# Reordering the beginning of a one-core Fourier-mixing and feed-forward kernel: store count, load order, and where a weight conversion runs

## The chip, the cores and the metric

One core of one Trainium2 chip runs the program. The metric is the device time of one execution in microseconds, lower is better. All runs quoted were in the fast state (in some executions of a program the chip shows a slower one). The kernel before takes 2857.4 us (median).

## The reference

Eight sequences of 3008 x 256 are filtered in the frequency domain; the result, 24064 rows, passes a feed-forward layer with a hard-swish.

```python
X = np.fft.rfft(x, axis=1)                       # x: (8, 3008, 256)
y = np.fft.irfft(X * (filt_r + 1j * filt_i)[None], n=3008, axis=1)
h = y.reshape(24064, 256) @ w_in                 # w_in: (256, 2048), float64
g = h * np.clip(h + 3.0, 0.0, 6.0) / 6.0
out = (g @ w_out).astype(np.float32)             # w_out: (2048, 256), float64
```

## The kernel before

The Fourier transform is done in two matmul stages, through two buffers in memory, z and g. For sequence 0 nothing can overlap, so the program begins with a prologue:

- **Stage A**: eight chunks of x are loaded (`x_load`), multiplied (`a_unit`), copied from PSUM (the memory that matmuls write) by ScalarE and stored to z (`z_store`).
- **Stage B**: z is read back (`t2_load`); twelve units of a matmul, the filter product in five VectorE instructions (`f_unit`, `y_unit`) and an inverse matmul (`bi_unit`); the result goes to g (`g_store`).
- **Bridge**: g is read back (`t4_load`), 40 matmuls (`n_unit`), the first up-projection.
- **Main loop**: 376 steps (47 blocks x 8 weight parts), each an up-projection, hard-swish and down-projection. The stages A and B of sequences 1 to 7 are strewn into it.

The weights arrive as 64-bit floats and are converted to 32 bits by integer instructions on VectorE, then scaled and combined on GpSimd (`w_conv`): sixteen pieces, two per weight part, the pieces of part p being needed by steps p and p + 1.

```python
def w_conv(i):                                   # ... hi, lo: the words of the 64-bit floats
    v.tensor_scalar(out=big, in0=hi, scalar1=3, scalar2=0x3FFFFFFF, ...)
    v.tensor_scalar(out=rest, in0=hi, scalar1=30, scalar2=30, ...)
    v.tensor_tensor(out=big, in0=rest, in1=big, op=ALU.bitwise_or)
    v.tensor_scalar(out=hi, in0=hi, scalar1=20, scalar2=0x7FF, ...)
    v.tensor_scalar(out=hi.bitcast(FP32), in0=hi, scalar1=897.0, op0=ALU.is_ge)
    # ... four more on VectorE; then on GpSimd a product and four sums
def z_store(b, c, q=None):
    # ... for g in range(2): for ri in range(2):
            for h in range(2):                   # 8 stores of 48 KB per chunk
                q.dma_start(z[:, h, ds(c * XC + 2 * g, 2), :], t[p0:p0 + KH, h, :, :])
# ... prologue:
for c in range(NB):                              # stage A
    a_unit(0, c)
    z_store(0, c, nc.scalar)
    if c + 3 < NB: x_load(0, c + 3)
    if c < 4: convert(1)                         # convert: w_conv, then the load of the next piece but one
for c in range(TB):
    table_load(0, c)                             # six loads, 1 MB
    t2_load(0, c, nc.gpsimd)
# ... stage B: convert(1) in every fourth unit
for i in range(2): t4_load(i)                    # eight loads of 120 KB
# ... n_unit x4
for i in range(NCONV - done): at(i // 2, convert, 1)   # nine left: two in each step
```

Of the kernel before, what the change touches and what calls it, by code (L numbers as in the profile page):

```python
# [10 lines left out]
FP32 = mybir.dt.float32  # L11
I32 = mybir.dt.int32
AXT = mybir.ActivationFunctionType
ALU = mybir.AluOpType
# [7 lines left out]
NC = 64  # L22
KH = 24
NF = N // 2 + 1
P = 128
# [4 lines left out]
HC = NC // 2  # L30
XC = 4
NB = HC // XC
TC = 4
NT = KH // TC
TB = 3
# [3 lines left out]
BLK = 512  # L39
NBLK = B * N // BLK  # L40
NJ = 5
RING = 3 * BLK


# [33 lines left out]
def kernel(  # L78
# [9 lines left out]
    nc = tc.nc  # L88
# [9 lines left out]
    g_d = nc.dram_tensor("g_tmp", (B, KH, P, D), FP32, kind="Internal").ap()  # L98

    def pool(name, bufs, **kw):  # L100
        return ctx.enter_context(tc.tile_pool(name=name, bufs=bufs, **kw))

    const = pool("const", 1)
# [11 lines left out]
    op = pool("op", 2)  # L115
# [6 lines left out]
    xs = [const.tile([P, XC, D], FP32, name="xs%d" % i) for i in range(3)]  # L122
    ft = [const.tile([P, TC, D], FP32, name="ft%d" % i) for i in range(TB)]
    t4 = [const.tile([P, NJ, D], FP32, name="t4%d" % i) for i in range(2)]
    xn = const.tile([P, 2, RING], FP32, name="xn")
    w_in = [const.tile([P, 7, P], FP32, name="w_in%d" % p) for p in range(NP)]
    w_out = [const.tile([P, 7, P], FP32, name="w_out%d" % p) for p in range(NP)]
    half_c = const.tile([P, 1], FP32, name="half_c")

    st = {}  # L130

    def raw(src, row, ap):
        return bass.AP(tensor=src.tensor, offset=src.offset + row * D, ap=ap)


    def table_load(b, c):
        t = ft[(b * NT + c) % TB]
        for src, p0 in ((filt_r, 0), (filt_i, HALF)):
            nc.sync.dma_start(t[p0:p0 + 32, :, :].rearrange("p k d -> p (k d)"),
                              raw(src, c * TC, [[NA * D, 32], [1, TC * D]]))  # L140
            nc.sync.dma_start(t[p0 + 32:p0 + 64, :, :], raw(src, NA - c * TC, [[NA * D, 32], [-D, TC], [1, D]]))
        wb = tabp.tile([P, TC, P], FP32, name="wb")
        nc.sync.dma_start(wb, wb_d[:, ts(c, TC), :])
        wi = tabp.tile([P, TC, P], FP32, name="wi")
        nc.sync.dma_start(wi, wi_d[:, ts(c, TC), :])
        st["tab", b, c] = wb, wi
# [8 lines left out]
    def w_part(i):  # L155
        p = i // 2
        if i % 2 == 0:
            cols = ts(p, 256)
            src = moe_w_in[:, cols].bitcast(I32)
            return src.rearrange("(a p) d -> p a d", p=P), w_in[p][:, 0:4, :].rearrange("p (a j) m -> p a (j m)", a=2)  # L160
        src = moe_w_out[ts(p, 2 * P), :].bitcast(I32)
        return src.rearrange("(a p) d -> p a d", p=P), w_out[p][:, 0:4, :].rearrange("p (a j) m -> p a (j m)", a=2)

    def w_load(i):
        if i >= NCONV:
            return
        t = op.tile([P, 1024], I32, name="bits", tag="o")
        nc.gpsimd.dma_start(t.rearrange("p (a d) -> p a d", a=2), w_part(i)[0])
        st["bits", i] = t

    def w_conv(i):
        if i >= NCONV:
            return
        words = st.pop(("bits", i)).rearrange("p (n two) -> p n two", two=2)
        lo, hi = words[:, :, 0], words[:, :, 1]
        big, rest = (sp.tile([P, 2, D], FP32, name=s).bitcast(I32).rearrange("p a n -> p (a n)")
                     for s in ("s1", "s2"))
        v = nc.vector
        v.tensor_scalar(out=big, in0=hi, scalar1=3, scalar2=0x3FFFFFFF,
                        op0=ALU.logical_shift_left, op1=ALU.bitwise_and)  # L180
        v.tensor_scalar(out=rest, in0=hi, scalar1=30, scalar2=30,  # L181
                        op0=ALU.logical_shift_right, op1=ALU.logical_shift_left)
        v.tensor_tensor(out=big, in0=rest, in1=big, op=ALU.bitwise_or)  # L183
        v.tensor_scalar(out=hi, in0=hi, scalar1=20, scalar2=0x7FF,
                        op0=ALU.logical_shift_right, op1=ALU.bitwise_and)
        v.tensor_scalar(out=hi.bitcast(FP32), in0=hi, scalar1=897.0, scalar2=None, op0=ALU.is_ge)
        v.tensor_scalar(out=rest, in0=big, scalar1=23, scalar2=23,
                        op0=ALU.logical_shift_right, op1=ALU.logical_shift_left)
        v.tensor_scalar(out=lo, in0=lo, scalar1=9, scalar2=0x3F800000,
                        op0=ALU.logical_shift_right, op1=ALU.bitwise_or)  # L190
        rest, big = rest.bitcast(FP32), big.bitcast(FP32)
        v.scalar_tensor_tensor(out=rest, in0=lo.bitcast(FP32), scalar=1.0, in1=rest,  # L192
                               op0=ALU.subtract, op1=ALU.mult)
        v.scalar_tensor_tensor(out=rest, in0=rest, scalar=2.0 ** -20, in1=big, op0=ALU.mult, op1=ALU.add)  # L194
        two = lambda t: t.rearrange("p (a d) -> p a d", a=2)
        nc.gpsimd.tensor_tensor(out=w_part(i)[1], in0=two(rest), in1=two(hi.bitcast(FP32)), op=ALU.mult)

        w = (w_in, w_out)[i % 2][i // 2]
        for o, x0, x1, op_ in IN_SUMS if i % 2 == 0 else OUT_SUMS:
            nc.gpsimd.tensor_tensor(out=w[:, o, :], in0=w[:, x0, :], in1=w[:, x1, :], op=op_)  # L200
# [36 lines left out]
            nc.scalar.activation(out=t[:, h, :, :], in_=ps[h], func=AXT.Copy)  # L237
        st["t1", b, c] = t

    def z_store(b, c, q=None):  # L240
        q = q or nc.gpsimd
        t = st.pop(("t1", b, c))
        for g in range(2):
            for ri in range(2):
                p0 = g * 64 + ri * 32
                z = z_d[b, :, ts(ri, NC), :].rearrange("k (h j) d -> k h j d", h=2)
                for h in range(2):
                    q.dma_start(z[:, h, ds(c * XC + 2 * g, 2), :], t[p0:p0 + KH, h, :, :])  # L248

    def t2_load(b, c, q=None):  # L250
        q = q or nc.sync
        t = t2p.tile([P, TC, D], FP32, name="t2")
        q.dma_start(t, z_d[b, ts(c, TC), :, :].rearrange("k p d -> p k d"))
        st["t2", b, c] = t
# [38 lines left out]
    def g_store(b, c, q=None):  # L293
        q = q or nc.gpsimd
        q.dma_start(g_d[b, ts(c, TC), :, :].rearrange("k p d -> p k d"), st.pop(("t3", b, c)))



    chunks = [(b, j, min(NJ, HC - j)) for b in range(B) for j in range(0, HC, NJ)]

# [1 line left out]
        b, j, n = chunks[i]  # L302
        return b * N + j * TOK, n * TOK

    def t4_load(i):
        b, j, n = chunks[i]
        for h in range(2):
            for ri in range(2):
                p0 = h * 64 + ri * 32
                nc.sync.dma_start(t4[i % 2][p0:p0 + KH, 0:n, :], g_d[b, :, ds(ri * NC + h * HC + j, n), :])  # L310


    def n_unit(i, dh):
# [5 lines left out]
        while done < n:  # L319
            o = (t + done) % RING  # L320
            m = min(n - done, RING - o)
            nc.scalar.activation(out=xn[:, dh, ds(o, m)], in_=ps[:, ds(done, m)], func=AXT.Copy)  # L322
# [144 lines left out]
    def at(step, fn, *a):  # L467
        plan.setdefault((step, fn in EARLY), []).append((fn, a))

    with tc.manual_schedule():  # L470



        nc.vector.memset(half_c, 0.5)
        for t in xs:
            nc.gpsimd.memset(t, 0.0)
        nc.sync.dma_start(wa, wa_d)
        for c in range(3):
            x_load(0, c)
# [4 lines left out]
        def convert(n):  # L484
            nonlocal done
            for _ in range(n):
                w_conv(done)
                w_load(done + 2)
                done += 1

        for c in range(NB):
            a_unit(0, c)
            z_store(0, c, nc.scalar)
            if c + 3 < NB:
                x_load(0, c + 3)
            if c < 4:
                convert(1)
        for c in range(TB):
            table_load(0, c)
            t2_load(0, c, nc.gpsimd)  # L500
        nc.sync.dma_start(wai, wai_d)
        for t in t4:
            nc.gpsimd.memset(t, 0.0)
        for i in range(NU + 1):
            if i < NU:
                b_unit(0, i)
                f_unit(0, i)
                y_unit(0, i)
                if i % 4 == 2:
                    convert(1)  # L510
            if i:
                bi_unit(0, i - 1)
                if i % 2 == 0:
                    c = i // 2 - 1
                    g_store(0, c, nc.scalar)
                    if c + TB < NT:
                        table_load(0, c + TB)
                        t2_load(0, c + TB, nc.gpsimd)
        for i in range(2):
            t4_load(i)  # L520
        for i in range(2):
            for dh in range(2):
                n_unit(i, dh)
# [1 line left out]
            x_load(1, c)  # L525

        for i in range(NCONV - done):
            at(i // 2, convert, 1)

        n_at = {0: -2, 1: -2}  # L530
        used = {}
# [131 lines left out]
```

## Time and profile before

| stretch of the trace | from, us | length, us | what fills it |
|---|---|---|---|
| stage A | 0 | 62.4 | DMA share 75%, every engine under 42% |
| stage B | 62.4 | 63.0 | VectorE 87% |
| bridge | 125.3 | 24.3 | a store, a load, then matmuls at a granted clock of 0.57 |
| steps 0 to 5 | 149.6 | 85.1 | VectorE 90% |
| the rest | 234.75 | 2620 | TensorE 99% |

The cuts are the first matmul of stage B, the end of its last VectorE result, the first addition into h of the main loop, and the same addition six steps later. In lines of the profile PE is TensorE, PEld its weight loads, DVE VectorE, ACT ScalarE, POOL GpSimd and SP SyncE; a q behind the name (ACTq) marks DMA issues of that queue.

### The profile page before, as it was taken

What the parts mean: (1) busy time and instruction counts of PE and PEld (TensorE: products, weight loads), DVE (VectorE), ACT (ScalarE), POOL (GpSimd) and SP (SyncE); (2) the same over time, 40 slices, a digit from 0 to 9 for tenths busy, and PEclk for the clock granted to TensorE, in tenths of its full rate; (3) what the DMA queues carried; (4) which work ended last, traced back from release to release, by engine and by line L of the source; (5) the groups of instructions that cost most, each with busy time, mean ns of one, the idle gap of its engine ahead of it and who ended that gap; (6) DMA issues with size and microseconds to landing.
All of it is one profiled execution on the core that took longest, in us unless ns stands there. A gap on an engine that the chain in (4) does not pass through costs nothing.

```text
span 2854.4 us, 47635 instructions
## 1 busy us (share of the span) xinstructions
PE 2726.7 (96%) x18096; PEld 2469.4 (87%) x18096; DVE 1995.0 (70%) x3492; ACT 1331.6 (47%) x2670; POOL 511.7 (18%) x836
## 2 busy tenths in 40 slices
PE   4569999999999999999999999999999999999997
PEld 1358988999989999899988999899998999999996
DVE  3687875677756777577765777567775677766665
ACT  1124445544554445544455444554455444444443
POOL 3274003200131001310123010320013100000000
PEclk9789999999999999999999999999999999999998
DMA  6544213421134212332223221332113421110000
GB/s 200 161 128 109 88 39 87 109 82 48 48 87 112 63 51 65 95 102 56 60 69 92 85 79 39 86 107 67 58 45 91 117 66 45 34 32 23 18 8 15
DMA packets 129323, 211.92 MB, mean 74 GB/s; under 512 B 26184, under 2 KB 87240, under 8 KB 129096
## 3 DMA queue, kind: packets, MB, share of 16 engines
q1 hardware_dynamic: 100072, 146.98, 18.5%
q0 software_dynamic: 23552, 55.62, 6.6%
q10 hardware_dynamic: 5472, 6.29, 0.7%
q8 instruction: 143, 2.34, 0.3%
q14 instruction: 84, 0.69, 0.1%
HBM read 133.81 MB, written 74.97 MB: 73 GB/s over the span
## 4 chain that ended last, share of the span: by engine, by line
PE 91%; DVE 5%; DMA 2%; issue 1%; ACT 1%; ACTq 0%; SPq 0%; POOL 0%; POOLq 0%; DVEq 0%
PE po L417 41%; PE al L341 22%; PE be L341 17%; PE psn L316 4%; PE psf L260 3%; PE psf L288 3%; PE psf L234 2%; DMA z_tmp<-t 1%; DVE g L391 0%; DVE s L183 0%; DVE s L192 0%; DVE s L194 0%; DVE s L181 0%; DVE g L398 0%; DVE s L274 0%
## 5 line engine op out<-in xcount | busy, mean ns | idle before, releaser
L417 PEld LDWEIGHTS po<-w_out,g 128*128 128x128 f32 x10528 | 1408.5, 192 | 146.1 <-DVE g L399 30.4
L417 PE MATMUL po<-w_out,g 128*128 128x128 f32 x10528 | 1433.9, 276 | 26.6 <-DVE g L391 26.2
L386 ACT ACTIVATE r<-h,half_c 128x512 f32<-128x512 f32 x752 | 542.7, 722 | 344.5 <-DVE h L367 332.3
L391 DVE SCALAR_TENSOR_TENSOR g<-r,h 128x512 f32<-128x512 f32 x752 | 517.2, 688 | 258.6 <-ACT r L386 245.5
L341 PE MATMUL al<-xt,w_in 128*128 128x256 f32 x2256 | 677.5, 382 | 3.2 <-DVE h L372 2.7
L367 DVE TENSOR_TENSOR h<-be,s 128x512 f32<-128x512 f32 x376 | 259.6, 691 | 285.8 <-PE be L341 258.4
L341 PE MATMUL be<-xn,w_in 128*128 128x256 f32 x1504 | 447.3, 379 | 0.0
L341 PEld LDWEIGHTS al<-xt,w_in 128*128 128x128 f32 x2256 | 344.0, 193 | 5.8 <-DVE h L372 3.0
L381 ACT ACTIVATE h<-al 128x256 f32<-128x256 f32 x376 | 144.5, 384 | 376.5 <-PE al L341 376.5
L341 PEld LDWEIGHTS be<-xn,w_in 128*128 128x128 f32 x1504 | 285.8, 190 | 38.8
L248 POOL DMA_DIRECT2D z_tmp<-t x448 | 226.0, 512 | 382.1 <-ACT t L237 373.0
L372 DVE TENSOR_TENSOR h<-al,s 128x256 f32<-128x256 f32 x376 | 159.4, 424 | 192.8 <-PE al L341 192.4
L399 DVE TENSOR_TENSOR g<-g 128x512 f32<-128x512 f32 x376 | 262.1, 697 | 12.9
L362 ACT ACTIVATE s<-al 128x256 f32<-128x256 f32 x376 | 144.5, 384 | 202.0 <-PE al L341 202.0
L353 ACT ACTIVATE s<-be 128x256 f32<-128x256 f32 x376 | 144.5, 384 | 180.4 <-PE be L341 180.4
L341 PE MATMUL al<-xn,w_in 128*128 128x256 f32 x752 | 225.6, 382 | 0.5 <-ACT h L381 0.5
L341 PE MATMUL be<-xt,w_in 128*128 128x256 f32 x752 | 223.9, 379 | 0.0
L352 ACT ACTIVATE s<-al 128x256 f32<-128x256 f32 x376 | 144.5, 384 | 71.0 <-PE al L341 71.0
L398 DVE TENSOR_TENSOR g<-g 128x256 f32<-128x256 f32 x376 | 164.9, 438 | 12.8
L401 DVE TENSOR_TENSOR g<-g 128x256 f32<-128x256 f32 x376 | 164.8, 438 | 12.8
L334 POOL TENSOR_TENSOR xt<-xn 128x256 f32<-128x256 f32 x94 | 72.0, 766 | 508.1 <-ACT xn L322 508.0
L341 PEld LDWEIGHTS be<-xt,w_in 128*128 128x128 f32 x752 | 143.3, 191 | 19.5
(50 smaller groups left out, 1816.5 us busy)
## 6 DMA issues: line engine op xcount, KB each, us to landing
t<-g_tmp SPq DMA_DIRECT2D x192, 120.0 KB
z_tmp<-t POOLq DMA_DIRECT2D x448, 48.0 KB, 2.3
t<-z_tmp SPq DMA_DIRECT2D x42, 512.0 KB
g_tmp<-t POOLq DMA_DIRECT2D x42, 512.0 KB, 3.4
xs<-in_x_dram SPq DMA_DIRECT2D x128, 128.0 KB
out_dram<-o SPq DMA_DIRECT2D x328, 47.0 KB
ft<-in_filt_r_dram SPq DMA_DIRECT2D x96, 128.0 KB
ft<-in_filt_i_dram SPq DMA_DIRECT2D x96, 128.0 KB
```

The costliest lines, as they stand in the source:

```text
L248: q.dma_start(z[:, h, ds(c * XC + 2 * g, 2), :], t[p0:p0 + KH, h, :, :])
L341: nc.tensor.matmul(ps, w_in[p][:, w, :], x, start=start, stop=stop, skip_group_check=True)
L352: nc.scalar.activation(out=s[:, 0, :], in_=al, func=AXT.Copy)
L353: nc.scalar.activation(out=s5, in_=be[:, 1, :], func=AXT.Copy)
L367: nc.vector.tensor_tensor(out=st["h"][0].rearrange("p (a n) -> p a n", a=2), in0=be, in1=s, op=ALU.add)
L372: nc.vector.tensor_tensor(out=st["h"][1][:, 256:512], in0=al, in1=s5, op=ALU.add)
L386: nc.scalar.activation(out=r, in_=st["h"][i], func=AXT.Relu, bias=half_c, scale=1.0 / 6.0)
L391: nc.vector.scalar_tensor_tensor(out=st["g", k, p][:, o:o + 2, :].rearrange("p a n -> p (a n)"), in0=st["r", i], scalar=1.0, in1=st["h"][i ...
L398: v.tensor_tensor(out=g[:, G1, :], in0=g[:, G3, :], in1=g[:, G22, :], op=ALU.add)
L399: v.tensor_tensor(out=g[:, G3:G2 + 1:2, :], in0=g[:, G3:G1 + 1, :], in1=g[:, G11:G11 + 1, :].broadcast_to([P, 2, 256]), op=ALU.subtract)
L401: v.tensor_tensor(out=g[:, G4, :], in0=g[:, G12, :], in1=g[:, G2, :], op=ALU.subtract)
L417: nc.tensor.matmul(st["po", k][bank][:, part, u, :], g[:, a, ts(u, P)], w_out[p][:, w, :], start=(p == 0 and n in OPENS and u == 0), stop= ...
```

## The change

Its intent is to shorten the prologue: fewer and larger z stores over two queues, z loads on the sync queue ahead of tables, a shorter conversion with one pass on ScalarE, and conversions spread so that no step of the loop has two.

```diff
+        v.scalar_tensor_tensor(out=big, in0=hi, scalar=top_c, in1=big,
+                               op0=ALU.bitwise_and, op1=ALU.bitwise_or)
+        high = hi.bitcast(FP32)
+        nc.scalar.activation(out=high, in_=high, func=AXT.Abs)
         # ... (four instructions that were here go)
+        v.tensor_scalar(out=high, in0=high, scalar1=SMALL, scalar2=None, op0=ALU.is_ge)
         # ... z_store:
-                for h in range(2):
-                    q.dma_start(z[:, h, ds(c * XC + 2 * g, 2), :], t[p0:p0 + KH, h, :, :])
+                q = qs[ri] if qs else nc.gpsimd
+                q.dma_start(z[:, :, ds(c * XC + 2 * g, 2), :], t[p0:p0 + KH, :, :, :])
         # ... prologue:
-        for t in xs:
-            nc.gpsimd.memset(t, 0.0)
+        for i, t in enumerate(xs):
+            (nc.vector, nc.gpsimd, nc.vector)[i].memset(t, 0.0)
         # ...
-            z_store(0, c, nc.scalar)
+            z_store(0, c, (nc.sync, nc.scalar))
             if c + 3 < NB:
                 x_load(0, c + 3)
-            if c < 4:
+            elif c + 3 == NB:
+                table_load(0, 0)
+            if c % 2:
                 convert(1)
         for c in range(TB):
-            table_load(0, c)
-            t2_load(0, c, nc.gpsimd)
+            t2_load(0, c)
+            if c:
+                table_load(0, c)
         # ... stage B:
-                if i % 4 == 2:
+                if i % 3 == 1:
                     convert(1)
         # ... also t2_load ahead of table_load here, on the sync queue
+                    if c == NT - 2:
+                        t4_load(0, 0, KH - TC)          # 20 of 24 rows, early
+                        t4_load(1, 0, KH - TC)
+        convert(2)
         for i in range(2):
-            t4_load(i)
+            t4_load(i, KH - TC)                         # the last 4 rows
         # ...
-            at(i // 2, convert, 1)
+            at(i, convert, 1)
```

More of the change, by code (lines that the diff above doesn't have):

```diff
@@ L41 @@
 NJ = 5
+SMALL = float(np.array(897 << 20, np.int32).view(np.float32))
 RING = 3 * BLK
@@ L128 @@
     half_c = const.tile([P, 1], FP32, name="half_c")
+    top_c = const.tile([P, 1], I32, name="top_c")
     st = {}
@@ L180, in w_conv @@
                         op0=ALU.logical_shift_left, op1=ALU.bitwise_and)
-        v.tensor_scalar(out=rest, in0=hi, scalar1=30, scalar2=30,
-                        op0=ALU.logical_shift_right, op1=ALU.logical_shift_left)
-        v.tensor_tensor(out=big, in0=rest, in1=big, op=ALU.bitwise_or)
-        v.tensor_scalar(out=hi, in0=hi, scalar1=20, scalar2=0x7FF,
-                        op0=ALU.logical_shift_right, op1=ALU.bitwise_and)
-        v.tensor_scalar(out=hi.bitcast(FP32), in0=hi, scalar1=897.0, scalar2=None, op0=ALU.is_ge)
+        v.scalar_tensor_tensor(out=big, in0=hi, scalar=top_c, in1=big,
+                               op0=ALU.bitwise_and, op1=ALU.bitwise_or)
+        high = hi.bitcast(FP32)
+        nc.scalar.activation(out=high, in_=high, func=AXT.Abs)
         v.tensor_scalar(out=rest, in0=big, scalar1=23, scalar2=23,
@@ L194, in w_conv @@
         v.scalar_tensor_tensor(out=rest, in0=rest, scalar=2.0 ** -20, in1=big, op0=ALU.mult, op1=ALU.add)
+        v.tensor_scalar(out=high, in0=high, scalar1=SMALL, scalar2=None, op0=ALU.is_ge)
         two = lambda t: t.rearrange("p (a d) -> p a d", a=2)
-        nc.gpsimd.tensor_tensor(out=w_part(i)[1], in0=two(rest), in1=two(hi.bitcast(FP32)), op=ALU.mult)
+        nc.gpsimd.tensor_tensor(out=w_part(i)[1], in0=two(rest), in1=two(high), op=ALU.mult)
         w = (w_in, w_out)[i % 2][i // 2]
@@ L238, in a_unit, with z_store @@
         st["t1", b, c] = t
-    def z_store(b, c, q=None):
-        q = q or nc.gpsimd
+    def z_store(b, c, qs=None):
         t = st.pop(("t1", b, c))
@@ L303, in token, with t4_load @@
         return b * N + j * TOK, n * TOK
-    def t4_load(i):
+    def t4_load(i, k0=0, k1=KH):
         b, j, n = chunks[i]
@@ L309, in t4_load @@
                 p0 = h * 64 + ri * 32
-                nc.sync.dma_start(t4[i % 2][p0:p0 + KH, 0:n, :], g_d[b, :, ds(ri * NC + h * HC + j, n), :])
+                nc.sync.dma_start(t4[i % 2][p0 + k0:p0 + k1, 0:n, :], g_d[b, k0:k1, ds(ri * NC + h * HC + j, n), :])
     def n_unit(i, dh):
@@ L474 @@
         nc.vector.memset(half_c, 0.5)
-        for t in xs:
-            nc.gpsimd.memset(t, 0.0)
+        nc.vector.memset(top_c, -0x40000000)
+        for i, t in enumerate(xs):
+            (nc.vector, nc.gpsimd, nc.vector)[i].memset(t, 0.0)
         nc.sync.dma_start(wa, wa_d)
@@ L516 @@
                     if c + TB < NT:
+                        t2_load(0, c + TB)
                         table_load(0, c + TB)
-                        t2_load(0, c + TB, nc.gpsimd)
+                    if c == NT - 2:
+                        t4_load(0, 0, KH - TC)
+                        t4_load(1, 0, KH - TC)
+        convert(2)
         for i in range(2):
-            t4_load(i)
+            t4_load(i, KH - TC)
         for i in range(2):
```

## The prediction

> **What bounds the kernel now.** I read the page's slices first. A slice is 2854.4 / 40 = 71.4 us.
>
> ```profile
> PE   4569999999999999999999999999999999999997
> DVE  3687875677756777577765777567775677766665
> PEclk9789999999999999999999999999999999999998
> DMA  6544213421134212332223221332113421110000
> ```
>
> TensorE is full from the fifth slice to the end; only the first four, some 240 us, have idle time. So the change, which is about the beginning, can win only there. I then cut the beginning at its first events (first matmul of the second stage at 62.37, last vector result of it at about 125.4, first vector instruction of the main loop at 149.64, the same instruction six steps later at 234.75) and asked for busy time by stretch:
>
> ```profile
> 0.00:62.37 62.37, 23.91 (x64) 4.80 (x65) 20.74 (x37) 9.97 (x17) 25.57 (x38) 1.00 0.75 219
> 62.37:125.46 63.09, 34.44 (x92) 21.81 (x93) 54.93 (x87) 6.57 (x11) 14.95 (x20) 0.81 0.44 143
> 125.46:149.64 24.18, 14.59 (x62) 11.95 (x62) 0.00 (x0) 4.98 (x10) 3.68 (x6) 0.57 0.63 170
> 149.64:234.75 85.11, 58.84 (x299) 45.37 (x300) 76.50 (x123) 25.08 (x50) 69.42 (x103) 0.82 0.41 111
> 400.00:2854.00 2454.00, 2433.14 (x16512) 2236.66 (x16511) 1711.71 (x3023) 1208.18 (x2429) 376.30 (x637) 1.00 0.23 66
> ```
>
> Columns: stretch and length, then busy us of PE, PEld, DVE, ACT, POOL, then granted clock, DMA share, GB/s. Stage A (0 to 62) has every engine under 42% and DMA at 75%. Stage B (to 125) is VectorE: 54.93 of 63. The bridge (to 150) has an idle VectorE. Steps 0 to 5 (85 us) are VectorE again, 76.5. Past 400 us TensorE is busy 99%.
>
> For stage A, the time order of ScalarE, its queue, and the waits of both queues:
>
> ```profile
> 8.23 4.99 ACTq L248 DMA_DIRECT2D z_tmp<-t  x8
> 13.90 4.10 ACTq L248 DMA_DIRECT2D z_tmp<-t  x8
> ...
> 43.85 4.63 ACTq L248 DMA_DIRECT2D z_tmp<-t  x8
> ...
> 49.21 3.29 ACTq L248 DMA_DIRECT2D z_tmp<-t  x8
> ...
> ACT t L237 <- DMA z_tmp<-t: 19.7, 4, 6.1
> ...
> SPq L224 <- DMA z_tmp<-t: 14.2, 9, 4.5
> ```
>
> Eight store issues fill nearly the whole interval between chunks, and even x loads wait for z stores (14.2 us). Loads don't read z: what they wait for is a semaphore. In the order of instructions each DMA of the two hardware queues waits for one of eight completion semaphores, dealt out in turn. So at most eight transfers are in flight, over both queues together. Chunks start (49.21 - 8.23) / 7 = 5.85 us apart, with 8 stores and 4 loads each, 12 transfers through 8 places: one transfer holds a place 5.85 x 8 / 12 = 3.9 us.
>
> For steps 0 to 3, the VectorE groups in 149.64 to 214:
>
> ```profile
> L181 DVE TENSOR_SCALAR s<-bits 128x512 int32<-128x512 int32 x8 | 7.7, 964 | 0.0
> L183 DVE TENSOR_TENSOR s<-s,s 128x512 int32<-128x512 int32 x8 | 6.1, 762 | 0.3
> L398 DVE TENSOR_TENSOR g<-g 128x256 f32<-128x256 f32 x4 | 5.6, 1388 | 0.1
> L179 DVE TENSOR_SCALAR s<-bits 128x512 int32<-128x512 int32 x8 | 3.4, 420 | 0.0
> ```
>
> L398 takes 425 ns later in the loop but 1388 here, and L181 964 where the same kind (L179) takes 420: they are blocked while GpSimd works on the previous conversion.
>
> **What the Trainium skill says.** "DMA: Bandwidth & Descriptors", section "Issuing engines are not separate DMA queues": a second issuing engine saves only the sequencer's issue time. The trace agrees as far as it goes: an issue is some 0.31 us of queue time, eight are 2.5 of 5.85 us, and the rest is waiting. So I credit the halved number of transfers, not the second queue. "SBUF — State Buffer", section "Who interferes with whom": VectorE in a 2-port mode, or with two SBUF inputs, shares a port pair with GpSimd, and the later one blocks. The 1388 against 425 ns agrees. "VectorE: DVE Perf Modes", section "Mode 2×_2P — use both read ports for one tensor": tensor_scalar in fp32 runs at twice the rate of tensor_tensor; the trace has 0.42 against 0.69 us, so the new three-input form should cost 0.69. "TensorE: Matmul & The Clock Gate", section "HAM oscillation — how this bites in real kernels": idle gaps beyond about 3.4 us make TensorE restart slowly. Here the granted clock of steps 0 to 5 is 0.82, after gaps of 4 to 7 us.
>
> **The change, part by part.**
> (1) *Stage A.* Four stores of 96 KB replace eight of 48 KB, with the same 2 KB pieces; so 4 + 4 = 8 transfers per chunk through 8 places, one turn of 3.9 us. Rate check: x 376 KB + z 384 KB per 3.9 us is about 200 GB/s, plus weights some 60; the slices inside stage A reach 300 to 330. I stretch 3.9 to 4.2 for it. The last three chunks have no x load behind them, only one table of six transfers: I take 3.5 each for the last two. Last stores issue at 8.3 + 5 x 4.2 + 2 x 3.5 = 36.3 and land about 4 later, 40.3. The z load (4.95 us before, three at a time through GpSimd) now goes first on the sync queue, its table already loaded: about 4.5. First stage-B matmul at 45 in place of 62.4: **17 saved**.
> (2) *Conversion.* Before: five tensor_scalar at 0.42-0.43, four others at 0.69, whose starts take 4.33 us undisturbed. After: four tensor_scalar and three scalar_tensor_tensor; starts 4 x 0.37 + 3 x 0.68 = 3.5, say 3.6. ScalarE gains one 128x512 pass, estimated at 0.6 from its other passes of that size; it is under half busy.
> (3) *Stage B.* Twelve units of five VectorE instructions at 3.61 = 43.3 either way. Before three conversions (13.3), after four (14.4, plus about 0.3 each of blocking); waits 4 before, about 3 after. 61 against 61: **0**.
> (4) *Bridge.* Two conversions run in the idle VectorE, 7.5 of 24 us: free. The t4 load is split: 20 of 24 rows arrive before the last g store. That load now takes from 131.4 to 136.7; with a sixth of the bytes but still about 2 us of latency and four issues, 3.8: **1.5 saved**. The GpSimd work of the two conversions is over before the first sums are due.
> (5) *Steps 0 to 5.* Before: nine conversions, two in each of steps 0 to 3 (16.1 us each), one in step 4 (12.0), none in step 5 (8.6); sum 85.1. Step 1 splits as 2.07 (h, h, first product) + 4.33 + 6.18 (second conversion, blocked by GpSimd) + 3.49 (second product and three sums, blocked too; 2.3 clean) = 16.07. After: one per step for six steps, 2.07 + 3.6 + 3.5 = 9.2. I take 9.8, because with 2 us gaps TensorE may still run below full clock (step 5 took 8.6 at 0.69), and because xt sums come in on GpSimd at step 4. 6 x 9.8 = 59 against 85: **26 saved**.
> (6) *Later steps.* GpSimd issues half the z stores; TensorE is full: **0**.
> Sum: 17 + 1.5 + 26 = 44.5; 2857.5 - 44.5 = **2813**.
>
> **The rivals.**
> (a) *Bandwidth takes the places' place.* If stage A was limited by bytes (219 GB/s on average), halving the count gives little: perhaps 6 saved instead of 17, total 2824. For it: DMA share 0.75. Against: slices of 300 GB/s and more inside the stage, and loads that wait for unrelated stores.
> (b) *A new wait in the steps.* GpSimd must finish a conversion (4.0), a load issue (0.8) and four z stores (2.3) = 7.1 of a 9.2 us step, and ScalarE's copy of chunk c + 2 waits until the stores of chunk c have landed, two steps later, with under 1 us of slack by my count. ScalarE would then stall ahead of the s copies; steps of 11 us, 7 us given back, total 2820. The new ScalarE pass adds to that order. Together with (a): 2831.
> (c) *All goes well.* Turns of 3.5 us in stage A (23 saved), steps of 8.9 (32 saved), bridge 3: 58, total 2799, just over 2%.
> (d) *Slower.* The sync queue now holds loads behind stores that wait for ScalarE; a bad order could cost stage A its gain. But its stores wait for the copies that also free the x buffers, so I see little chance.
>
> **Range and chances.** The middle is 2813. Either rival alone stays below 2826, both together reach 2831; (c) is 2799. I take 2802 to 2828 for eight in ten. Over 2% faster is below 2801.5 and needs nearly everything in (c): 0.10. Slower by 2% would need 57 us lost where the work shrinks: 0.01. Within 2%: 0.89.
>
> **What the profile of the changed kernel would show.** Step 1: z store issues about 4 us apart, first stage-B matmul at 41 to 49; at 55 or later the bandwidth rival holds. Step 2: seven VectorE instructions per conversion, 3.5 to 3.8 us. Step 3: stage B still 60 to 66 long. Step 4: the bridge 22 to 23. Step 5: h additions (L368 in the new file) 9 to 10.5 us apart over six steps; at 11 or more, look for ScalarE waiting on z stores. Step 6: the rest unchanged within 3 us. The prediction is wrong most likely in (1), if a place is held much shorter or longer than 3.9, or in (5).

## The result, and the profile after

The changed kernel takes **2827.65 us** (2826.72 to 2828.85) against 2857.44 in the same rounds: 29.8 us or 1.05% less, which is clear of the noise. The ratio is 0.9895, 95% interval 0.9878 to 0.9912. A ratio is the mean time of one kernel's fast runs over that of the other's of the same rounds, so not quite the ratio of the medians. In the two profiled runs the spans differ by 2854.4 - 2827.1 = 27.3 us.

The same view of busy time by stretch, for the changed kernel with its own cuts:

```profile
0.00:56.36 56.36, 23.80 (x65) 4.87 (x65) 19.20 (x32) 12.61 (x21) 21.65 (x33) 1.00 0.70 203
56.36:121.88 65.52, 43.83 (x92) 26.74 (x92) 57.11 (x88) 8.80 (x15) 17.18 (x23) 0.85 0.62 183
121.88:149.77 27.89, 15.54 (x62) 12.44 (x62) 7.85 (x15) 6.32 (x12) 11.39 (x18) 0.55 0.69 184
149.77:208.57 58.80, 52.13 (x312) 39.27 (x313) 54.27 (x84) 27.88 (x56) 42.22 (x57) 0.97 0.45 127
```

Compare the lengths (second column): stage A is 6.0 us shorter, stage B 2.6 longer, the bridge 3.6 longer, steps 0 to 5 26.3 shorter. So step 0 begins at 149.77, where it began at 149.64 before: what stage A won was spent before the loop started, and the whole gain of the trace lies in six steps. (In a repeat of the same kernel, "changed, again" below, step 0 began at 147.19, so up to 2.4 us of this differs from trace to trace.) Their granted clock rose from 0.82 to 0.97.

Stage A, ScalarE's queue in time order (start, length, engine, line, count):

```profile
13.07 0.91 ACTq L249 DMA_DIRECT2D z_tmp<-t  x2
...
32.83 0.76 ACTq L249 DMA_DIRECT2D z_tmp<-t  x2
39.28 0.87 ACTq L249 DMA_DIRECT2D z_tmp<-t  x2
44.94 0.88 ACTq L249 DMA_DIRECT2D z_tmp<-t  x2
```

The first five intervals average (32.83 - 13.07) / 5 = 3.95 us, which looks like the turn of 3.9 that the prediction derived. But the first two of them are 3.16 each, the pace of a chunk's matmuls (2.5) and the wait for a copy (0.7), with x already loaded; the next three are 5.4, 4.6 and 3.4. The first store is at 13.07, not 8.2, and the last two intervals are 6.5 and 5.7. All seven average 4.55.

The prediction's premise holds in the kept traces. Their semaphore events, which none of these views lists, show that in each of the fourteen runs the DMAs of the two hardware queues (sync and scalar) signal just eight semaphores, and that up to 60 us none was issued before the last one on its semaphore had landed. In the kernel before, a place then stood free for 0.09 us (median) before it was used again.

Why the first is late: GpSimd, then TensorE, then the stretch from 4 to 8 us by busy time, before and after. First the kernel before:

```profile
3.41 0.87 POOL L168 DMA_DIRECT2D bits<-in_moe_w_in_dram  x1
...
4.67 2.90 PE L234 MATMUL psf<-xs,wa 64*64 64x512 f32 x8 [4.67 <-DMA xs<-in_x_dram]
...
4.00:8.00 4.00, 2.90 (x8) 0.61 (x8) 0.00 (x0) 0.40 (x1) 0.99 (x2) 1.00 0.92 261
```

And the changed kernel:

```profile
1.63 0.85 POOL L170 DMA_DIRECT2D bits<-in_moe_w_in_dram  x1
...
9.95 1.98 PE L236 MATMUL psf<-xs,wa 64*64 64x512 f32 x6 [1.00 <-DMA xs<-in_x_dram]
...
4.00:8.00 4.00, 0.98 (x2) 0.29 (x2) 1.35 (x3) 0.00 (x0) 0.00 (x0) 1.00 1.01 310
```

With two of its three memsets moved to VectorE, GpSimd issues the first weight loads (1 MB) at 1.63 instead of 3.41, ahead of the first x load at 2.02. From 4 to 8 us the DMA engines are full (share 1.01) and the first chunk of x is complete only at 9.95.

### The profile page after: what moved, and what is told of

It reads as the page before. It is cut to its first block, busy times and chain, and to the rows that moved or that the text cites. A ratio compares the mean times of both kernels' runs of the same rounds, so it can differ in the third digit from the quotient of the medians.

```text
span 2827.1 us, 47246 instructions
## 1 busy us (share of the span) xinstructions
PE 2728.8 (97%) x18096; PEld 2467.2 (87%) x18096; DVE 1981.8 (70%) x3463; ACT 1340.4 (47%) x2686; POOL 411.1 (15%) x604
## 4 chain that ended last, share of the span: by engine, by line
PE 92%; DVE 4%; DMA 2%; ACT 1%; issue 1%; POOL 0%; SPq 0%; POOLq 0%; ACTq 0%; DVEq 0%
PE po L418 41%; PE al L342 23%; PE be L342 17%; PE psn L317 4%; PE psf L261 3%; PE psf L289 3%; PE psf L236 2%; DMA z_tmp<-t 1%; DVE g L392 0%; DVE g L399 0%; DVE s L183 0%; DVE s L193 0%; DVE s L275 0%; DVE h L368 0%; DVE s L274 0%
## 5 line engine op out<-in xcount | busy, mean ns | idle before, releaser
L400 DVE TENSOR_TENSOR g<-g 128x512 f32<-128x512 f32 x376 | 261.4, 695 | 12.9
L249 POOL DMA_DIRECT2D z_tmp<-t x224 | 132.5, 596 | 422.6 <-ACT t L239 419.5
L317 PEld LDWEIGHTS psn<-wai,t 128*128 128x128 f32 x1024 | 135.4, 197 | 18.1 <-POOL w_out L202 12.5
```

The lines of the kernel that those rows point to most:

```text
L317: nc.tensor.matmul(ps[:, ts(q, TOK)], t4[i % 2][:, q, ts(dh, P)], wai, start=True, stop=True)
L400: v.tensor_tensor(out=g[:, G3:G2 + 1:2, :], in0=g[:, G3:G1 + 1, :], in1=g[:, G11:G11 + 1, :].broadcast_to([P, 2, 256]), op=ALU.subtract)
```

## The experiments

All are alterations of the changed kernel unless said otherwise; all gave correct results. In the table "stage A" is the first matmul of stage B; the last columns are medians and the ratio to the kernel before of the same rounds.

| run | stage A | stage B | bridge | steps 0-5 | us (before) | ratio |
|---|---|---|---|---|---|---|
| before | 62.4 | 63.0 | 24.3 | 85.1 | 2857.4 | 1 |
| changed | 56.4 | 65.5 | 27.9 | 58.8 | 2827.7 (2857.4) | 0.9895 |
| changed, again | 56.5 | 63.7 | 27.1 | 59.2 | 2826.2 (2858.3) | 0.9887 |
| weight loads later | 54.6 | 64.3 | 28.2 | 59.0 | 2825.8 (2858.6) | 0.9886 |
| t4 load whole | 53.9 | 64.6 | 23.8 | 59.2 | 2825.4 (2858.6) | 0.9881 |
| no conversion in the bridge | 57.2 | 64.4 | 25.5 | 58.8 | 2839.4 (2858.6) | 0.9932 |
| bridge's weight loads later | 55.6 | 64.8 | 23.9 | 60.3 | 2825.4 (2858.6) | 0.9883 |
| eight z stores | 63.4 | 64.6 | 27.1 | 58.9 | 2834.5 (2856.3) | 0.9924 |
| z stores on one queue | 52.3 | 65.5 | 27.7 | 58.9 | 2822.9 (2856.3) | 0.9883 |
| table after the z stores | 54.5 | 64.4 | 27.3 | 58.9 | 2824.5 (2856.3) | 0.9887 |
| old conversion | 56.8 | 66.7 | 23.8 | 61.8 | 2829.1 (2856.3) | 0.9903 |
| combined | 48.0 | 64.4 | 24.5 | 58.9 | 2817.2 (2858.3) | 0.9859 |
| before + spreading only | 65.7 | 65.8 | 25.0 | 63.2 | 2844.5 (2858.3) | 0.9950 |
| before + four stores only | 59.0 | 63.9 | 24.1 | 83.6 | 2852.4 (2857.9) | 0.9980 |

The five runs whose stage A is coded as in the changed kernel and whose VectorE work is the same (changed, again, t4 whole, no bridge conversion, bridge's loads later) reach stage B between 53.9 and 57.2. So a single trace tells stage A only to some 3 us. The totals of runs of different rounds can be compared only by their ratios, whose intervals are about 0.0015, or 4 us, to each side: of the single alterations of the changed kernel, only "no conversion in the bridge" has a total clear of the changed kernel's own, and "eight z stores" all but.

### The start of stage A

```diff
+        for t in t4: nc.gpsimd.memset(t, 0.0)     # moved here from below
         w_load(0)
         w_load(1)
```

> The changed kernel, with the two t4 memsets of GpSimd moved ahead of its first two weight loads, so that these start about 2.3 us later. Theory (the weight loads, now 1.8 us earlier than in the kernel before, take the DMA engines from the first x loads): the first matmuls on the whole of x chunk 0 start at about 5 us instead of 9.95, the first z store issues at about 9 instead of 13.07, the first stage-B matmul comes 3 to 5 us earlier than 56.4, and the total falls by 3 to 5 us to about 2823. Rival (the x loads are late by their own memsets on VectorE or by the issue on the sync queue): nothing moves by more than 1 us.

```profile
9.25 0.92 ACTq L249 DMA_DIRECT2D z_tmp<-t  x2
...
42.55 0.95 ACTq L249 DMA_DIRECT2D z_tmp<-t  x2
```

The first z store issued at 9.25 instead of 13.07 (12.97 to 13.37 in the five runs): shown, the weight loads had held up the first chunk. But the last store issued at 42.55, 2.4 us earlier, and stage B started at 54.6, inside the spread. Most of the early gain was absorbed further on: the seven intervals took 33.3 us, 4.76 each, where they took 31.9 before. So with stores on two queues this cause alone is worth 2 us or less, and the total doesn't settle it.

### The number of stores, the queues, and the table

```diff
-                q.dma_start(z[:, :, ds(c * XC + 2 * g, 2), :], t[p0:p0 + KH, :, :, :])
+                for h in range(2):      # stage A only
+                    q.dma_start(z[:, h, ds(c * XC + 2 * g, 2), :], t[p0:p0 + KH, h, :, :])
```

> The changed kernel with eight z stores of 48 KB per chunk in stage A again, but over the two queues. Theory 'places' (eight transfers in flight over both hardware queues; 12 transfers per chunk then take 12/8 turns): z store groups come about 5.5 to 6 us apart again (4.0 over the first five chunks of the changed kernel), stage B starts 6 to 9 us later than the 54 to 57 of the runs so far, total 2833 to 2837. Rival 'queue' (what helps is the second issuing queue): intervals stay near 4 to 4.6, stage B starts within 2 us, total within 2 us.

```profile
12.54 1.80 ACTq L250 DMA_DIRECT2D z_tmp<-t  x4
...
47.91 1.86 ACTq L250 DMA_DIRECT2D z_tmp<-t  x4
```

With the same bytes over the same two queues, eight stores per chunk brought stage B to 63.4, 7 us later, as late as before the change. Intervals rose to (47.91 - 12.54) / 7 = 5.05, from 4.55 over the same seven (4.28 in the repeat) and less than the 5.5 expected. So ScalarE's last store came 3 us later; the rest of the 7 us is on the sync queue, where the z load was issued at 59.37. By the semaphore events a 48 KB store held its place for 2.5 us on average, one of 96 KB in the changed kernel 3.7: half the bytes, more than half the time. The number of transfers matters; the second queue doesn't make up for it.

```diff
-            z_store(0, c, (nc.sync, nc.scalar))
+            z_store(0, c, (nc.scalar, nc.scalar))
```

> The changed kernel with all four z stores of a chunk on the scalar queue, none on the sync queue. Theory 'places': the same within 2 us, perhaps 1 us earlier since x loads no longer queue behind stores. Rival 'queue': stage B starts 3 us or more later.

One queue was not worse but better: stage B at 52.3, below every run with two, though only 1.6 us below the lowest of the five, and the total doesn't settle it. The combined kernel below does: it differs from "weight loads later" in stage A by this edit alone, and there stage B starts 6.6 us earlier (48.0 against 54.6). The likely reason is in the expectation: loads no longer stand behind stores. On the sync queue of the changed kernel (start, length, count), the last stores take 7.2 us to issue, behind the table's loads, and the z load follows at 50.62:

```profile
40.82 0.43 SPq L147 DMA_DIRECT2D wi<-wi_t  x1
41.34 7.19 SPq L249 DMA_DIRECT2D z_tmp<-t  x4
50.62 0.94 SPq L254 DMA_DIRECT2D t<-z_tmp  x2
```

With one queue for the stores, the same queue has no stores, the table is issued by 37.89, and the z load goes at 48.33:

```profile
37.89 0.43 SPq L147 DMA_DIRECT2D wi<-wi_t  x1
48.33 0.92 SPq L254 DMA_DIRECT2D t<-z_tmp  x2
```

The table itself was tried next:

```diff
-            elif c + 3 == NB:
-                table_load(0, 0)
 ...
+        table_load(0, 0)
         for c in range(TB):
             t2_load(0, c)
```

> The changed kernel with the first table's six loads issued after the last z store of stage A instead of between chunks 5 and 6 (still ahead of the z loads on the same queue). Theory (the table loads stand in the sync queue ahead of the stores of chunks 6 and 7 and hold places, which is why the last two intervals are 6.5 and 5.7 us and not 3.5): the last two intervals fall to about 4, the last z store lands 3 to 4 us earlier, stage B starts 1 to 4 us earlier. Rival (the last intervals are long because of x loads or weight loads): the intervals stay near 6, and stage B starts as late or later, since the table still has to come.

The last two intervals went from 6.5 and 5.7 to 6.5 and 3.6. That doesn't show the last one to be the table's: in the repeat of the changed kernel, with the table in its old place, it was 3.15.

```profile
40.15 0.72 ACTq L249 DMA_DIRECT2D z_tmp<-t  x2
43.30 2.50 ACTq L249 DMA_DIRECT2D z_tmp<-t  x2
```

What lies outside the spread is the z load: it was issued at 47.33 (50.0 to 51.6 in the five runs), so the table's loads had held up the last stores of the sync queue. But the table's loads then stood just ahead of it, the first matmul followed 7.2 us later instead of 5.7, and stage B at 54.5 is within the spread. Why the interval before is some 6 us in all these runs isn't explained.

The kernel before with only this part of the change:

```diff
-                for h in range(2):
-                    q.dma_start(z[:, h, ds(c * XC + 2 * g, 2), :], t[p0:p0 + KH, h, :, :])
+                q.dma_start(z[:, :, ds(c * XC + 2 * g, 2), :], t[p0:p0 + KH, :, :, :])
```

> The kernel before with one alteration: the z stores of a chunk are four of 96 KB (everywhere), still on the scalar queue in stage A. Theory 'places': z store groups 4 to 4.6 us apart instead of 5.85, stage B starts at 50 to 55 instead of 62.4, stages B, bridge and steps unchanged, total 8 to 12 us under the kernel before. Rival (bytes set the pace of stage A, and the gain of the changed kernel there comes from its other parts): stage B starts at 60 or later, total within 3 us.

A miss: stage B at 59.0, 3.4 us gained, total -5.5. Its chain of waits shows what took the place of the stores (start, length, what):

```profile
33.55 5.84 DMA z_tmp<-t
39.41 5.04 DMA ft<-in_filt_i_dram
44.47 4.77 DMA z_tmp<-t
49.63 3.33 DMA ft<-in_filt_r_dram
52.98 5.95 DMA t<-z_tmp
```

Its x loads were done sooner, so the sync queue went on to three tables, 3 MB, while stores of chunks 6 and 7 were still to come. Table loads (L139 to L145) and z stores then waited for one another in turn, 5 us at a time. Fewer stores need the reordered loads behind them to pay.

### The bridge

```diff
-                    if c == NT - 2:
-                        t4_load(0, 0, KH - TC)
-                        t4_load(1, 0, KH - TC)
-            t4_load(i, KH - TC)
+            t4_load(i)
```

> The changed kernel with the t4 load in one piece again, after the last g store. Theory A (the bridge of 27.9 us is longer than the 24.3 of before because two extra weight loads share the DMA engines with the last g store and the t4 load): the bridge becomes no shorter, 28 to 30 us, total 2827 to 2830. Theory B (the split into 16 small loads is what lengthened it): the bridge returns to about 24 us, total about 2824.

The bridge fell to 23.8, where the six runs with split and conversions unaltered took 27.1 to 28.2: theory B, the split.

```diff
-        convert(2)        # the other conversions move to steps 0 to 7
```

> The changed kernel without the two conversions of the bridge: steps 0 to 7 take one conversion each instead of steps 0 to 5. Theory A (the weight loads that these conversions bring delay the g store and the t4 load): the bridge falls from 27.9 to about 24 us or less; two more steps take 9.4 instead of 6.8 us (+5), total about 2829. Theory B (split load): the bridge stays near 28, total about 2832.

The bridge fell to 25.5, half-way. The total is 10 us worse than expected: step 6 took 14.55 us, since the conversion at its end is needed by step 7 at once (TensorE waited 4.6 us for GpSimd's w_in there). That cost was not foreseen.

```diff
-        convert(2)
+        w_conv(done); w_conv(done + 1)      # their loads: after the n_units
-                if i % 3 == 1:
+                if i % 3 == 0:
```

> The changed kernel with the same two conversions in the bridge, but the weight loads that follow them are issued only after the bridge's matmuls are queued, and the conversions of stage B come one unit earlier, so that the load after the last of them is over before the last g store. Theory A (contention of weight loads with the g store and the t4 load): the last g store lands in about 3.3 us instead of 5.4 and the bridge falls to 23 to 25 us, total about 2823 to 2825. Theory B (split load): no change beyond 1 us.

The bridge fell to 23.9 with the split kept: theory A, the weight loads. (The edit moves the last weight load of stage B too, to 6.7 us ahead of the last g store instead of 2.6.) Both theories hold, then, because the delay needs both. The chain of waits tells how. Whole load in the kernel before:

```profile
128.17 3.22 DMA g_tmp<-t
...
132.72 3.87 DMA t<-g_tmp
```

No conversions in the bridge: the split load is quick, the last g store (beside the early part of the t4 load and one weight load) slow:

```profile
124.42 5.42 DMA g_tmp<-t
...
130.86 2.71 DMA t<-g_tmp
```

Weight loads later: both quick:

```profile
123.19 3.60 DMA g_tmp<-t
...
127.82 2.79 DMA t<-g_tmp
```

In the changed kernel itself, the sync queue and GpSimd:

```profile
119.67 13.11 SPq L311 DMA_DIRECT2D t<-g_tmp  x16
...
122.14 0.75 POOL L170 DMA_DIRECT2D bits<-in_moe_w_out_dram  x1
129.74 0.75 POOL L170 DMA_DIRECT2D bits<-in_moe_w_in_dram  x1
```

| | last g store, issue to landing | from there to the first matmul that reads t4 |
|---|---|---|
| before | 3.2 | 5.3 |
| changed | 5.4 | 5.8 |
| t4 load whole | 3.1 | 4.9 |
| no conversion in the bridge | 5.4 | 3.9 |
| bridge's weight loads later | 3.6 | 3.9 |

The g store (issued at 124.73) is slow where the early t4 loads and a weight load (issued at 122.14) are under way; take either away and it lands in 3.1 to 3.6. That weight load belongs to the last conversion of stage B, so it is there without the bridge's conversions too, and the kernel before has one as close ahead of its store (125.58 against 128.17, landed in 3.2): what is new is the early t4 part. The last four rows come in 3.9, as predicted, except where a second weight load, released by the bridge's first conversion, was issued just ahead of them (129.74 against 130.1). This gives 2.2 + 0.5 of the 3.6 us; the remaining 0.9 lies between the first of the 40 matmuls and the first addition, 13.9 against 12.9 us (13.1 in the repeat), and wasn't isolated. A warning on the view: it names GpSimd's w_out as what ended TensorE's 11.82 us wait for these matmuls, but they read t4 and a table. The DMA behind it has to be looked up by hand.

### Conversion: shorter, or elsewhere

```diff
-        v.scalar_tensor_tensor(out=big, in0=hi, scalar=top_c, in1=big, ...)
-        nc.scalar.activation(out=high, in_=high, func=AXT.Abs)
-        v.tensor_scalar(out=high, in0=high, scalar1=SMALL, ...)
+        # the four instructions of the kernel before
```

> The changed kernel with the conversion of the kernel before (nine VectorE instructions, none on ScalarE), all other parts kept. Theory (spreading the conversions, not shortening them, gives most of the gain in steps 0 to 5): steps of about 10.2 us instead of 9.4, six of them 5 us longer; stage B about 3 us longer (four conversions at 0.8 us); total about 2835. Rival (the shorter conversion is what matters): steps of 12 us, as step 4 of the kernel before, total 2845 or more.

Steps of 9.92 instead of 9.4 us, 3.0 over six; stage B 66.7 against 63.7 and 65.5. So shortening is worth 3 us in the steps and 1 to 3 in stage B. By the ratios the total rose only 2.3 to 4.6 us, which is not clear of the noise; in this run's trace the bridge did without the collision above (23.8). Its early t4 loads were all issued 6.8 us ahead of the last g store, against 2.5 in the changed kernel, and the store landed in 3.1: it depends on when the loads happen to fall.

```diff
-            if c < 4:                          # in the kernel before
+            if c % 2:
-                if i % 4 == 2:
+                if i % 3 == 1:
+        convert(2)
-            at(i // 2, convert, 1)
+            at(i, convert, 1)
```

> The kernel before with only the conversions' places altered (chunks 1, 3, 5, 7; every third unit; two in the bridge; one in each of steps 0 to 5), with its old nine-instruction conversion, its eight z stores and its whole t4 load. Theory (spreading is worth most of the 30 us): steps 0 to 5 take 61 to 62 us instead of 85; stage B 3 to 5 us longer; the bridge 24 to 25; stage A unchanged at 62; total 19 to 22 us under the kernel before. Rival (the three parts of the change need one another): under 12 us.

Steps 0 to 5 fell by 21.9 us to 63.2, as expected, so spreading is what shortens them. But the total fell only 13.9: stage A became 3.4 longer, stage B 2.8, and step 6 took 9.75 us where the kernel before has 7.4. In stage A the z store intervals late in the stage became 7 us; why was not tried. Theory and rival are both half right: the gain of spreading is there alone, but without the other parts a third of it goes elsewhere.

### All that helped, together

```diff
+        for t in t4: nc.gpsimd.memset(t, 0.0)          # ahead of the weight loads
+            z_store(0, c, (nc.scalar, nc.scalar))
+            t4_load(i)                                 # whole, no early part
```

> The changed kernel with three alterations tried singly before: weight loads behind the t4 memsets (first run), t4 load in one piece (second), all z stores on the scalar queue (sixth). If their gains add: stage B starts at about 51 (56.4), the bridge takes 24 (27.9), steps 0 to 5 unchanged at 58.8, total 7 to 9 us under the changed kernel of the same rounds, about 2819. If they overlap (the places and the weight loads set the pace anyway): 4 to 6 us under it.

> The changed kernel itself, unaltered, on the chip of the two runs below, to compare with: 2826 to 2829, about 30 us under the kernel before; stage B starts between 54 and 57 us.

2817.2 against 2826.2 for the changed kernel in the same rounds: 9.0 us less, 41 under the kernel before; the intervals of the ratios (0.9845 to 0.9872, and 0.9874 to 0.9901) do not meet. No overlap of the gains shows. Stage B starts at 48.0. The first stores now come close together, and the early start is no longer lost:

```profile
9.22 1.77 ACTq L249 DMA_DIRECT2D z_tmp<-t  x4
13.27 1.67 ACTq L249 DMA_DIRECT2D z_tmp<-t  x4
16.69 1.58 ACTq L249 DMA_DIRECT2D z_tmp<-t  x4
...
38.19 1.71 ACTq L249 DMA_DIRECT2D z_tmp<-t  x4
```

## Why the prediction was right or wrong

The measured time lies in the predicted range by a third of a microsecond, and in the most likely class. The middle, 2813, is 14.7 us too low. That the range held is partly luck: two of the three gains failed, by 11 and 5 us, and the range was just wide enough. Term by term:

1. **Stage A, "17 saved": wrong, 6.0.** The terms that were off: first store "8.3", measured 13.07 (+4.8), since I looked at the moved memsets as free and not at the weight loads that they release; the seven intervals "5 x 4.2 + 2 x 3.5" = 28.0, measured 31.9 (+3.9); landing "about 4", measured about 5.2 (+1.2); z load "4.5", measured 6.3 (+1.8). That makes 11.6, by rounding, and leads from 44.8 to 56.4. Two steps failed. The start was taken over from the kernel before, 8.3. And the sync queue, which got stores and loads in turn, was given no cost; rival (d) named it but saw "little chance".

   With stores on the scalar queue alone and the weight loads later (combined), the first store was at 9.22, the seven intervals took 28.97, and stage B started at 48.0, 3 us from the predicted 45. With the weight loads later alone they took 33.3. In all, they took 28.3 and 29.0 in the two runs with one queue, 29.9 to 33.3 in the eight with two queues and four stores. So the predicted turns were reached only without stores on the sync queue; the 3.95 of the first five intervals was no confirmation of it. The late start and the queue together are shown to cost 8.4 us of stage A; singly the start is inside the spread and the queue just outside it. Rival (a), bandwidth, came to the same number, 6 saved, and the prediction's own sign for it, 55 or later, came true. But its reason is refuted as the main one: the combined kernel moves the same bytes 8 us faster. The sign was a poor one, since another cause gives it too. From 4 to 8 us, where the loads crowd, bytes do count.
2. **Conversion, "3.6": nearly right.** In stage B it took 3.83 us from its first start to the start of what follows (65.62 to 69.45), against 4.37 in the kernel before (167.80 to 172.17): 0.5 us saved each, not 0.7, which fits steps of 9.92 and 9.4. The three-input form took 0.75 for the new instruction, 0.69 expected. (The prediction miscounts the nine old instructions: they are six tensor_scalar and three others.)
3. **Stage B, "0": off by 0.7 to 2.6** in two runs of the same kernel. The prediction's own terms add up to 60.6 before and 61.9 after, so they give 1.3 and not 0; and stage B before was 63. VectorE's busy time rose from 54.9 to 57.1. In the profiled run one unit waited 1.34 us for a filter table, a wait that I had not considered.
4. **Bridge, "1.5 saved": wrong, 3.6 lost.** The split did what was predicted (3.9 us from the g store's landing to the matmul) where nothing disturbed it. Two steps failed. The early part of the t4 load was given no cost, but it met the last g store, beside a weight load of stage B: 2.2 us. And the two conversions are not "free": I counted their VectorE time and not the weight loads that they trigger, the first of which held up the last four rows: 5.8 against 3.9, 1.9 us. With the 0.9 that wasn't isolated this makes, but for 0.1, the 5.1 between forecast and result.
5. **Steps 0 to 5, "26 saved": right, 26.3.** Steps took 9.4, 9.4, 9.5, 9.5, 11.7 and 9.4 us. TensorE kept its clock (0.97) better than I feared, so the 9.8 was reached by the one long step instead. In that step a wait of rival (b)'s kind shows, in the changed kernel between 185 and 200 us:

```profile
ACT t L239 <- DMA z_tmp<-t: 4.9, 1, 4.9
```

   ScalarE waited 4.9 us for z stores to land; the step is 2.3 us over its neighbours. The sums of xt run on GpSimd in the same step, and the two were not taken apart.
6. **Later, "0": right** within 1.1 us in the traces.

(The best case (c) has a slip too: turns of 3.5 us save 21 in stage A by the prediction's own sum, not 23.) In all, the profiled gain is 6.0 - 2.6 - 3.6 + 26.3 + 1.1 = 27.2, by rounding 27.3.

## What to carry to other kernels

When work moves off an engine in the start-up, list what that engine issues next: here freed memsets and an added conversion each released a load that took the DMA engines from the transfer on the critical path, and a load that was split to start early met a store. Where completion semaphores are dealt out in turn, count transfers as well as bytes, and don't queue loads behind stores. An interval's mean can agree with a forecast by chance: look at its parts, and at a repeat, before calling it confirmed. A conversion that fills the bounding engine is best spread so that each step can hide it, but its last piece must be ready a step ahead of use.

## What the Trainium skill lacked or had wrong

- "Perfetto Trace Analysis", section "DMA Optimizations", says that splitting DMAs may let the task complete sooner if the engines are generally idle. The bridge shows what happens where they are not (DMA share 0.69): the split t4 load was quicker by itself (3.9 against 5.3 us) but the bridge grew to 27.9 us with it and was 23.8 without, as its early part met a store and a weight load. So this agrees with the page. The same section's advice to give loads and stores an issuing engine each agrees with the runs: 52.3 against 56.4 us to stage B, and 48.0 against 54.6 with the weight loads later.
- No page treats the number of completion semaphores as a limit on transfers in flight. The traces show eight for the two hardware queues. With the same bytes, eight stores per chunk instead of four cost 7 us of stage A (63.4 against 56.4), on two queues as well; how much of it is the wait for places and how much a fixed cost of each transfer was not taken apart.
- "SBUF — State Buffer", section "Who interferes with whom": nothing to mend. A VectorE sum with two inputs took 1410 ns beside GpSimd in steps 0 to 5 and 425 later on.
